# Reading a broadcast scalar through 16 partitions and a ones matmul, in a streaming multiply-add

## The chip, the core and the metric

The kernel runs on one core of a Trainium2 chip. The metric is the device time of one execution in microseconds; the kernel before takes 153.68 us (median of three runs, 153.3 to 153.85). A core has five engines that matter here: TensorE (PE) for matrix multiplications, VectorE (DVE) and ScalarE (ACT) for elementwise work, GpSimd (POOL), and SyncE (SP), which only issues transfers. Transfers between the device's memory and the on-chip memory SBUF (128 partitions) run on 16 DMA engines. SyncE and ScalarE each feed them through a queue of their own, q1 and q10 in this profile. PSUM is the small memory into which TensorE writes its results.

## The reference

```python
B, S, D = 512, 32, 640
x:  (512, 32, 640) bfloat16
fx: (512, 32, 640) bfloat16
alpha: (1,) bfloat16

def reference(x, fx, alpha):
    return x + alpha * fx
```

Each of the three large arrays has 10,485,760 elements, that is 20.97 MB. The kernel has to read two of them and write one, 62.9 MB in all, and does one multiply-add for each element.

## The kernel before

The three arrays are seen as 128 partitions of 81,920 elements each, and this row is cut into K = 5 chunks of 16,384 elements (`CHUNK`). One chunk of one array is 128 x 16,384 x 2 bytes, 4.19 MB, with 32,768 contiguous bytes for each partition.

For chunk k, `load_x(k)` and `load_f(k)` bring x and fx into SBUF tiles `x_t` and `f_t`. `compute(k)` is one VectorE instruction, `scalar_tensor_tensor`, that forms f_t * a_f + x_t and writes it over x_t (line 65). `store(k)` writes x_t to the output. There are four buffers for x_t and two for f_t, so a load of fx for chunk k has to wait until chunk k - 2 has been computed, and the load of x for chunk 4 until chunk 0 has been stored. The last chunk is computed and stored in two halves.

The order of the instructions is written out by hand (lines 81 to 101) and no scheduler changes it. All loads and stores are issued by SyncE in that order, except x of chunk 0, which ScalarE issues: SyncE's queue therefore has alpha, f0, x1, f1, x2, and then, as the computations end, f2, store 0, x3, f3, store 1, x4, f4 and the other stores. A queue passes transfers on in this order, and an issue that has to wait for a buffer holds up those after it on the same engine.

The scalar alpha is needed on all 128 partitions, as the operand `a_f` of each multiply-add. The function `alpha_to_lanes` (line 16) makes it: a transfer on SyncE, ahead of all others, reads the same two bytes once for each of the 128 partitions into `a_b` (line 20), and a VectorE copy turns them into float32 (line 22). Line numbers of 104 and above belong to the start and end of the program.

Of the kernel before, what the change touches and what calls it, by code (L numbers as in the profile page):

```python
# [1 line left out]

# [4 lines left out]

ACT = mybir.ActivationFunctionType
ALU = mybir.AluOpType
F32 = mybir.dt.float32  # L10
BF16 = mybir.dt.bfloat16

CHUNK = 16384


def alpha_to_lanes(nc, consts, alpha, eng):

    P = nc.NUM_PARTITIONS
    a_b = consts.tile([P, 1], alpha.dtype, name="a_b")
    eng.dma_start(out=a_b[:], in_=alpha.to_broadcast((P, 1)))  # L20
    a_f = consts.tile([P, 1], F32, name="a_f")
    nc.vector.tensor_copy(out=a_f[:], in_=a_b[:])  # L22
    return a_f


@with_exitstack
def kernel(
    ctx: ExitStack,
    tc: tile.TileContext,
    x: bass.AP,  # L30
    fx: bass.AP,
    alpha: bass.AP,
    out: bass.AP,
):
    nc = tc.nc
    P = nc.NUM_PARTITIONS
    xv = x.flatten_outer_dims().rearrange("(p n) d -> p (n d)", p=P)
    fxv = fx.flatten_outer_dims().rearrange("(p n) d -> p (n d)", p=P)
    ov = out.flatten_outer_dims().rearrange("(p n) d -> p (n d)", p=P)
    F = xv.shape[1]  # L40
    K = F // CHUNK
    assert K * CHUNK == F and K == 5

    consts = ctx.enter_context(tc.tile_pool(name="consts", bufs=1))
    xs = ctx.enter_context(tc.tile_pool(name="xs", bufs=4))
    fs = ctx.enter_context(tc.tile_pool(name="fs", bufs=2))
    ctx.enter_context(tc.manual_schedule())

    a_f = alpha_to_lanes(nc, consts, alpha, nc.sync)
    xt, ft = {}, {}  # L50

    def load_x(k):
        xt[k] = xs.tile([P, CHUNK], x.dtype, tag="x", name="x_t")
        eng = nc.scalar if k == 0 else nc.sync
        eng.dma_start(out=xt[k][:], in_=xv[:, bass.ts(k, CHUNK)])

    def load_f(k):
        ft[k] = fs.tile([P, CHUNK], fx.dtype, tag="f", name="f_t")
        nc.sync.dma_start(out=ft[k][:], in_=fxv[:, bass.ts(k, CHUNK)])

    def compute(k, parts=1):
        n = CHUNK // parts
        for j in range(parts):
            s = bass.ts(j, n)
            nc.vector.scalar_tensor_tensor(  # L65
                out=xt[k][:, s],
                in0=ft[k][:, s],
                scalar=a_f[:],
                in1=xt[k][:, s],
                op0=ALU.mult,  # L70
                op1=ALU.add,
            )

    def store(k, j=0, parts=1):
        n = CHUNK // parts
        nc.sync.dma_start(
            out=ov[:, k * CHUNK + j * n : k * CHUNK + (j + 1) * n],
            in_=xt[k][:, bass.ts(j, n)],
        )

    load_x(0)
    load_f(0)
    load_x(1)
    load_f(1)
    load_x(2)
    compute(0)
    load_f(2)
    store(0)
    load_x(3)
    compute(1)  # L90
    load_f(3)
    store(1)
    load_x(4)
    compute(2)
    load_f(4)
    store(2)
    compute(3)
    store(3)
    compute(4, 2)
    store(4, 0, 2)  # L100
    store(4, 1, 2)


# [1 line left out]
_INS = ['x', 'fx', 'alpha']  # L105
_OUTS = [((512, 32, 640), 'bfloat16')]


# [23 lines left out]
```

## Time and profile before

| | |
|---|---|
| median of three runs | 153.68 us |
| the profiled execution | 153.68 us |
| its span, first to last instruction | 151.9 us |
| VectorE: four multiply-adds of 128 x 16,384 | 69.1 us, 17.28 each |
| VectorE: two multiply-adds of 128 x 8,192 | 17.4 us, 8.75 each |
| VectorE: copy of alpha to float32 | 0.15 us, at 14.73 |
| VectorE idle until alpha has landed | 14.7 us |
| VectorE idle until an f_t has landed | 38.2 us in five waits |
| bytes read and written | 41.94 MB and 20.97 MB |
| TensorE | no compute instruction |

The idle times are those that ended with the landing named: VectorE had nothing else to do meanwhile. An idle engine costs nothing by itself; what counts is whether the end of the kernel hangs on it. The mean rate of the transfers over the span is 414 GB/s, and the page's slices give the rate over time, in 40 parts of 3.8 us each.

### The profile page before, as it was taken

The page shows a single profiled execution, that of the slowest core. Times are in us where ns is not written, and L with a number is a line of the kernel's source. Part 1 is how long each engine was busy: PE and PEld are TensorE (multiplying, and loading weights), DVE is VectorE, ACT ScalarE, POOL GpSimd, SP SyncE. Part 2 cuts the span into 40 slices and gives each one's busy share as a digit, 9 for nine tenths or more (in the row PEclk, how much of TensorE's full clock was granted, in tenths as well). Part 3 has the DMA queues.
Part 4 walks back from the last instruction along what each step waited for, and adds up shares of the span by engine and source line. Part 5 has one row for each costly group of instructions (what it writes and reads, how often), then busy time and mean ns, then how long its engine had stood idle before and what let it go on. Part 6 is the DMA issues. An engine that isn't in the chain of part 4 may idle for free.

```text
span 151.9 us, 81 instructions
## 1 busy us (share of the span) xinstructions
DVE 86.7 (57%) x7; POOL 0.2 (0%) x4
## 2 busy tenths in 40 slices
DVE  0000005999949999499992005999900089997000
POOL 0000000000000000000000000000000000000000
DMA  6988999999999999999999999999999999999993
GB/s 216 440 328 345 440 423 431 414 440 449 431 440 431 431 414 423 449 449 431 431 423 423 423 414 449 449 431 423 431 423 414 431 466 449 423 423 397 431 419 168
DMA packets 2448, 62.92 MB, mean 414 GB/s; under 512 B 400, under 2 KB 400, under 8 KB 400
## 3 DMA queue, kind: packets, MB, share of 16 engines
q1 hardware_dynamic: 2304, 58.72, 89.9%
q10 hardware_dynamic: 144, 4.19, 7.2%
HBM read 41.94 MB, written 20.97 MB: 414 GB/s over the span
## 4 chain that ended last, share of the span: by engine, by line
DMA 57%; DVE 29%; DVEq 6%; SPq 0%; issue 0%
DMA f_t<-in_fx_dram 57%; DVE x_t L65 29%; DVEq L127 6%; SPq L20 0%; DVEq L65 0%
## 5 line engine op out<-in xcount | busy, mean ns | idle before, releaser
L65 DVE SCALAR_TENSOR_TENSOR x_t<-f_t,a_f,x_t 128x16384 bf16<-128x16384 bf16 (+1 forms) x6 | 86.5, 14439 | 38.2 <-DMA f_t<-in_fx_dram 38.2
L22 DVE CAST a_f<-a_b 128x1 f32<-128x1 bf16 x1 | 0.2, 153 | 14.7 <-DMA a_b<-in_alpha_dram 14.7
L116 POOL MEMSET const-bfloat16-1.0<- 128x1 bf16 x1 | 0.1, 101 | 0.0
L116 POOL MEMSET const-uint8-127<- 128x1 uint8 x1 | 0.1, 101 | 0.0
L116 POOL MEMSET const-float32-0.0<- 128x1 f32 x1 | 0.1, 98 | 0.2 <-issue 0.2
L116 POOL MEMSET const-float32-1.0<- 128x1 f32 x1 | 0.1, 98 | 0.0
## 6 DMA issues: line engine op xcount, KB each, us to landing
f_t<-in_fx_dram SPq DMA_DIRECT2D x5, 4096.0 KB, 31.6
x_t<-in_x_dram SPq DMA_DIRECT2D x4, 4096.0 KB, 39.6
out_dram<-x_t SPq DMA_DIRECT2D x4, 4096.0 KB, 36.0
x_t<-in_x_dram ACTq DMA_DIRECT2D x1, 4096.0 KB, 13.3
out_dram<-x_t SPq DMA_DIRECT2D x2, 2048.0 KB, 13.3
a_b<-in_alpha_dram SPq DMA_DIRECT2D x1, 0.2 KB, 14.0
```

The costliest lines, as they stand in the source:

```text
L22: nc.vector.tensor_copy(out=a_f[:], in_=a_b[:])
L65: nc.vector.scalar_tensor_tensor(out=xt[k][:, s], in0=ft[k][:, s], scalar=a_f[:], in1=xt[k][:, s], op0=ALU.mult, op1=ALU.add,)
L116: nc = _bacc.Bacc("TRN2", target_bir_lowering=False, num_devices=1)
L127: with _tile.TileContext(nc) as tc:
```

## The change

Alpha is now read to 16 partitions instead of 128, by a transfer that ScalarE issues instead of SyncE. One row of it, a single element, is the moving operand of a matmul whose stationary operand is a row of 128 ones, set by VectorE; the product, alpha on 128 partitions, lies in PSUM as float32, and the VectorE copy into `a_f` reads it from there. The load of x for chunk 0 moves from ScalarE's queue to the head of SyncE's; the order of SyncE's other issues is the same. The tiles, the buffers, the multiply-adds and the stores are not touched.

```diff
-def alpha_to_lanes(nc, consts, alpha, eng):
+def alpha_to_lanes(nc, consts, psum, alpha, eng):
 
     P = nc.NUM_PARTITIONS
-    a_b = consts.tile([P, 1], alpha.dtype, name="a_b")
-    eng.dma_start(out=a_b[:], in_=alpha.to_broadcast((P, 1)))
+    a_1 = consts.tile([16, 1], alpha.dtype, name="a_1")
+    eng.dma_start(out=a_1[:], in_=alpha.to_broadcast((16, 1)))
+    ones = consts.tile([1, P], alpha.dtype, name="ones")
+    nc.vector.memset(ones[:], 1.0)
+    a_ps = psum.tile([P, 1], F32, name="a_ps")
+    nc.tensor.matmul(a_ps[:], ones[:], a_1[0:1, :], start=True, stop=True)
     a_f = consts.tile([P, 1], F32, name="a_f")
-    nc.vector.tensor_copy(out=a_f[:], in_=a_b[:])
+    nc.vector.tensor_copy(out=a_f[:], in_=a_ps[:])
     return a_f
...
+    psum = ctx.enter_context(tc.tile_pool(name="psum", bufs=1, space=bass.MemoryType.PSUM))
...
-    a_f = alpha_to_lanes(nc, consts, alpha, nc.sync)
+    a_f = alpha_to_lanes(nc, consts, psum, alpha, nc.scalar)
...
-        eng = nc.scalar if k == 0 else nc.sync
-        eng.dma_start(out=xt[k][:], in_=xv[:, bass.ts(k, CHUNK)])
+        nc.sync.dma_start(out=xt[k][:], in_=xv[:, bass.ts(k, CHUNK)])
```

## The prediction

> **What bounds the kernel now.** I read the page's summary and slices first, since they say which resource is full; then the chain of waits, which says what the end hangs on; then the rate of the DMA engines stretch by stretch, which says where the full resource is not full.
>
> ```profile
> span 151.9 us, 81 instructions
> ...
> DVE 86.7 (57%) x7; POOL 0.2 (0%) x4
> ...
> DMA  6988999999999999999999999999999999999993
> ...
> DMA packets 2448, 62.92 MB, mean 414 GB/s; under 512 B 400, under 2 KB 400, under 8 KB 400
> ```
>
> The only compute engine with work, VectorE, is busy for 57% of the span. The DMA engines read 9 in all slices but the first four (6988) and the last. The last line also says what the alpha read is made of. The kernel issues 17 transfers; if each ends in one small packet on each of 16 engines (the semaphore), that makes 272, and 400 - 272 = 128 packets are left: one 2-byte packet for each partition of a_b, eight on each engine.
>
> The chain of waits, in order of time, of which I show the first part and the end (start us, us, what):
>
> ```profile
> 1.32 23.12 DMA f_t<-in_fx_dram
> ...
> 24.58 17.30 DVE x_t L65
> ...
> 41.89 21.41 DMA f_t<-in_fx_dram
> ...
> 63.39 17.30 DVE x_t L65
> ...
> 80.70 41.33 DMA f_t<-in_fx_dram
> ```
>
> The chain puts 29% on VectorE, but this is a link of time, not a limit. While the multiply-add of tile 0 runs from 24.58 to 41.87, x1, f1 and x2 (three transfers of 4.19 MB) are queued already, 9.7 us each at 432 GB/s, so that the queue runs dry at about 24.5 + 29.1 = 53.6, and f2, the store of tile 0 and x3 join it at 41.9, some 12 us early. So the transfers are one long line, and the bytes set its length. What stands idle in that line is lost; where it is idle is in the table of stretches (columns: stretch, its length, busy time of DVE and of POOL, clock, DMA share, GB/s):
>
> ```profile
> 3.00:5.00 2.00, 0.00 (x0) 0.00 (x0) 1.00 0.95 410
> 5.00:7.00 2.00, 0.00 (x0) 0.00 (x0) 1.00 0.88 377
> 7.00:15.00 8.00, 0.15 (x1) 0.00 (x0) 1.00 0.91 356
> 15.00:31.00 16.00, 6.42 (x1) 0.00 (x0) 1.00 1.01 434
> 31.00:47.00 16.00, 13.90 (x2) 0.00 (x0) 1.00 1.00 432
> 47.00:79.00 32.00, 29.86 (x2) 0.00 (x0) 1.00 1.00 431
> 143.00:149.00 6.00, 0.00 (x0) 0.00 (x0) 1.00 1.01 431
> ```
>
> From 15 us to the end of the stores the engines hold 431 to 434 GB/s, and I take 432 as full. From 7 to 15 us they move 356. That is 8 x (432 - 356)/432 = 1.41 us of the whole line lost there. In the same time alpha and x_0 share the engines, as the page's issues show:
>
> ```profile
> x_t<-in_x_dram ACTq DMA_DIRECT2D x1, 4096.0 KB, 13.3
> ...
> a_b<-in_alpha_dram SPq DMA_DIRECT2D x1, 0.2 KB, 14.0
> ```
>
> Alpha's 256 bytes take 14.0 us from issue to landing and the 4 MB of x_0 13.3 us, against 9.7 us for a transfer of that size at 432 GB/s. The packet records of the trace show how: on each engine three packets of x_0 go first, then one of alpha and one of x_0 in turn. The first two of alpha cost nothing visible (the next 32 KB packet again takes 1.21 us), from the third on x_0's packets take 1.3 to 1.6 us. At the end, near 13 us, alpha's last two or three small packets go through with little beside them, and f_0, queued behind them on the same queue, has not started. That is the hole of 12 to 14 us.
>
> **What the Trainium skill says.** "DMA: Bandwidth & Descriptors", section "Queues, rings and completion order", states that each DMA engine takes the queues that have work in turn, packet by packet; the records agree, one alpha packet to one of x_0. The section "Why a DMA increments its semaphore by 16 and not by 1" gives the number of engines that share a transfer: the largest number up to 16 that divides the slowest dimensions of both sides. So 16 partitions get 16 engines, one element each; the 128 small packets of before (eight per engine) fit that, and no run yet shows the 16-row form. The section "Issuing engines are not separate DMA queues" states that transfers of different issuers run on the same 16 engines, so that moving x_0 from ScalarE's queue to SyncE's buys no bandwidth; the trace agrees, as its rate after 15 us, with SyncE alone issuing, is the 432 above.
>
> **The change part by part.** The sum is made against the profiled execution: 153.68 us, of which 151.9 is the span and 1.8 lies around it. The median of the runs shown is the same 153.68.
>
> *Alpha's read, 128 packets to 16.* Eight 2-byte packets per engine become one. Its cost before is the 1.41 us of the stretch from 7 to 15. What one costs is not shown by itself. Lower bound: nothing, since the first two alpha packets on each engine cost nothing and the 4-byte semaphore packets later lie in the stream without lowering 432. Upper bound: the loss of 3 to 7 us as well was alpha's (2 x 22/432 + 2 x 55/432 = 0.36 us) and returns in full. I take 0. Removed: 1.41 us. Were all of 3 to 15 us alpha's, it would be 1.77.
>
> *Alpha moved to ScalarE's queue, x_0 to SyncE's.* SyncE issues x_0 first, in the place of alpha, then f_0, x_1, f_1, x_2 as before: still five issues at the start, so nothing later is issued later. Alpha's first issue on SyncE took 0.54 us (0.72 to 1.26), x_0's on ScalarE 0.36 (0.73 to 1.09). If SyncE takes 0.54 for x_0, its data starts 0.17 us later; if 0.36, not at all. I take +0.10. All transfers of x and fx are now on one queue, and the engines go from x_0 to f_0 as they go from f_0 to x_1 in before, where the table shows no loss.
>
> *The work added: memset of a 1 x 128 row, weight load and matmul of one column, copy out of PSUM.* None is in the trace of before except the copy (0.153 us, from SBUF); the small memsets of GpSimd took 0.10. For the matmul, "TensorE: Matmul & The Clock Gate", section "Part 2: What happens when you issue a matmul", prices one of N columns at the low clock at (219 + N)/1.2 ns, 0.18 us here, which no run yet shows. By these an estimate of the chain is 0.1 + 0.18 + 0.15, about half a microsecond after alpha lands; with the waits between the engines I allow 2 us. VectorE's first multiply-add waits for x_0 and f_0, which land near 23 us. If alpha lands by 7 us (behind three packets of x_0, the worst order that the trace shows), a_f is ready by 9 with 14 us to spare, and if alpha stayed as late as 14.7 there would still be 6. The matmul waits for alpha and the copy for the matmul; behind the copy on VectorE stands only the multiply-add of tile 0, which would delay f_2 and the store of tile 0, whose issue has those 12 us of cover. Cost: 0. On TensorE, and on ScalarE behind its one issue, nothing is queued.
>
> *What is late next.* Nothing new: the line moves as a whole. f_0 lands 1.3 us earlier, tile 0 ends earlier, f_2 is issued earlier by the same, and the last store too, because each issue has its cover in a full queue (the last half store is issued at 139.7 and the other stores are under way until about 146).
>
> Sum: 153.68 - 1.41 + 0.10 + 0 = 152.37, said as 152.4; with the other bounds 151.9 (1.77 removed, no later start) to 152.9 (1.41 removed, 0.36 and 0.17 back).
>
> **The rivals.**
> *Half of it stays.* One small read per engine still upsets the stream at the start, when x_0's first packets are being waited for. For it: those first packets took 1.7 to 2.4 us, so the start is delicate. Against: two alpha packets in the middle cost nothing. 153.68 - 0.7 = 153.0.
> *No change.* The hole is made by passing from one queue to the other with a small transfer between, whatever its count, or only some engines gain while the slowest stays. For it: the end is set by the slowest of 16 engines, and the last packets of the engines end 1.4 us apart. Against: x_0's packets are slowed well before the passage. 153.6.
> *Slower: SyncE's queue starts late.* Alpha was issued on SyncE's queue at 0.72, yet its first packet runs 4.1 us after the first of x_0, which was issued on ScalarE's at 0.73. If that is the queue's own start and not its turn behind x_0, x_0 now pays it: 153.68 - 1.41 + 4.1 = 156.4. It makes the kernel slower once the late start is more than 1.41 + 0.46 = 1.9 us. Against: alpha enters on every engine exactly after its third x_0 packet, staggered like those packets, which looks like turns behind read-ahead.
> *The change does not do what it says.* Were the 16 reads put on one engine, that engine would have twice the small packets of before, and lose about 2.8 us instead of 1.4: 155.1.
>
> **How the numbers follow.** Full gain, 152.4: 0.60. Half, 153.0: 0.18. No change, 153.6: 0.12. Late queue, 156.4: 0.07. One engine, 155.1: 0.03. A difference of 0.3% (0.46 us) is what a measurement can tell, so faster means under 153.22 and slower over 154.14. Faster: 0.60 and most of the half case, 0.75; same: the rest of that case and the third, 0.15; slower: 0.10. Range: 151.6 (a little under the lower bound, for the spread of the runs, 153.3 to 153.85) to 153.5, which leaves out the slower cases and part of the third.
>
> **What would show it.** Right: 288 packets under 512 B in place of 400; alpha landing within some 7 us; x_0 landing near 11 to 12 us, f_0 and the first multiply-add near 23; 7 to 15 us at about 432 GB/s; all later landings shifted by the same 1.3 us. Wrong: first data after 3 us (late queue), 7 to 15 us still below 400 (no gain), or the early gain there and the last store no earlier (then the bytes are not the line that I take them for).

## The result, and the profile after

| | before | after |
|---|---|---|
| median of four runs each | 153.65 us (153.3 to 153.85) | 152.84 us (152.58 to 152.95) |
| ratio | | 0.9947, 95% interval 0.9925 to 0.997 |
| the profiled execution, its span | 153.68, 151.9 us | 152.80, 151.0 us |

The changed kernel is 0.8 us faster in these runs. A second series, 22 runs of it beside 67 of the kernel before, gave 0.9965 (0.995 to 0.9979), some 0.5 us. The forecast was 152.4, a gain of 1.3 us, so the direction held and the gain is about half of it.

The page of the kernel after, its summary, its slices and its packets:

```profile
span 151.0 us, 85 instructions
...
DMA  6999999999999999899999999999999999998994
GB/s 208 443 434 434 425 417 417 434 443 451 443 434 434 417 417 399 347 460 434 425 434 417 417 417 425 451 469 434 417 443 417 417 425 425 460 469 360 425 443 187
DMA packets 2336, 62.92 MB, mean 417 GB/s; under 512 B 288, under 2 KB 288, under 8 KB 288
```

There are 288 small packets instead of 400, 112 fewer, as 16 reads in place of 128 have to give. The slices at the start are full now: 6999 where before read 6988. But the rates show two low values that the kernel before has nowhere in its middle: 399 and 347, the slices from 56.6 to 64.2 us.

The same in the table of stretches, first before, then after (stretch, its length, busy time of each engine that works, clock, DMA share, GB/s; a packet counts in the stretch in which it starts, so only long stretches are sharp):

```profile
7.00:15.00 8.00, 0.15 (x1) 0.00 (x0) 1.00 0.91 356
15.00:48.00 33.00, 21.32 (x2) 0.00 (x0) 1.00 1.00 434
48.00:72.00 24.00, 21.86 (x2) 0.00 (x0) 1.00 1.00 433
72.00:148.00 76.00, 43.37 (x4) 0.00 (x0) 1.00 1.00 429
```

```profile
7.00:15.00 8.00, 0.16 (x1) 0.00 (x0) 0.16 (x1) 0.00 (x0) 1.00 1.04 446
15.00:48.00 33.00, 0.00 (x0) 0.00 (x0) 23.04 (x2) 0.00 (x0) 1.00 1.00 432
48.00:72.00 24.00, 0.00 (x0) 0.00 (x0) 20.84 (x2) 0.00 (x0) 1.00 1.01 415
72.00:148.00 76.00, 0.00 (x0) 0.00 (x0) 42.67 (x4) 0.00 (x0) 1.00 1.00 430
```

From 7 to 15 us the hole is filled, 446 for 356. From 48 to 72 us there is a new one: 24 x (433 - 415)/433 = 1.0 us.

The chain of waits after, in order of time, shows what this does to the line of transfers:

```profile
1.17 21.55 DMA f_t<-in_fx_dram
...
22.84 17.30 DVE x_t L69
...
40.16 22.44 DMA f_t<-in_fx_dram
...
62.69 17.29 DVE x_t L69
...
80.00 41.03 DMA f_t<-in_fx_dram
...
121.22 8.75 DVE x_t L69
```

The first multiply-add starts at 22.84, 1.74 us earlier than before (24.58). The third starts at 62.69, only 0.70 earlier (63.39): f_2 takes 22.44 us from its issue where it took 21.41. So more than half of the early gain is given back on the way to f_2. By the last chunk the lead is 1.0 us, against this line of the chain before:

```profile
122.22 8.75 DVE x_t L65
```

Of it 0.9 us is in the span of this execution; how far single executions differ is seen under e4.

The new path of alpha is harmless, as the timeline after shows (start, length, engine, line, operation; in brackets the idle time before it and what ended it):

```profile
0.73 0.57 ACTq L20 DMA_DIRECT2D a<-in_alpha_dram  x1
0.73 0.38 SPq L59 DMA_DIRECT2D x_t<-in_x_dram  x1
...
8.19 0.16 PE L24 MATMUL a_ps<-a,ones 1*128 1x1 bf16 x1 [8.19 <-DMA a<-in_alpha_dram]
8.38 0.16 DVE L26 COPY a_f<-a_ps 128x1 f32<-128x1 f32 x1 [7.41 <-PE a_ps L24]
```

Alpha lands just before 8.2 us, and 0.35 us later a_f is there, 14.3 us before the first multiply-add can use it. The issue of x_0 takes SyncE 0.38 us, and by the packet records its first data starts at 1.74 us, where before it was 1.73.

### The profile page after: what moved, and what is told of

It reads as the page before. It is cut to its first block, busy times and chain, and to the rows that moved or that the text cites. A ratio compares the mean times of both kernels' runs of the same rounds, so it can differ in the third digit from the quotient of the medians.

```text
span 151.0 us, 85 instructions
## 1 busy us (share of the span) xinstructions
PE 0.2 (0%) x1; PEld 0.1 (0%) x1; DVE 86.9 (58%) x8; POOL 0.2 (0%) x4
## 4 chain that ended last, share of the span: by engine, by line
DMA 56%; DVE 29%; DVEq 6%; issue 0%; SPq 0%
DMA f_t<-in_fx_dram 56%; DVE x_t L69 29%; DVEq L131 6%; SPq L59 0%; DVEq L69 0%
```

## The experiments

For all of them one measure is read from the timelines: the start of the first multiply-add, and the distance from the second to the third. Between these two lie the landings of f_1 and f_2, that is two transfers of 4.19 MB, 19.4 us at 432 GB/s; what is over 19.4 was lost on the way. Before and after:

```profile
43.96 17.28 DVE L65 SCALAR_TENSOR_TENSOR x_t<-f_t,a_f,x_t 128x16384 bf16<-128x16384 bf16 x1 [2.10 <-DMA f_t<-in_fx_dram]
...
63.39 17.29 DVE L65 SCALAR_TENSOR_TENSOR x_t<-f_t,a_f,x_t 128x16384 bf16<-128x16384 bf16 x1 [2.14 <-DMA f_t<-in_fx_dram]
```

```profile
42.24 17.28 DVE L69 SCALAR_TENSOR_TENSOR x_t<-f_t,a_f,x_t 128x16384 bf16<-128x16384 bf16 x1 [2.11 <-DMA f_t<-in_fx_dram]
...
62.69 17.28 DVE L69 SCALAR_TENSOR_TENSOR x_t<-f_t,a_f,x_t 128x16384 bf16<-128x16384 bf16 x1 [3.16 <-DMA f_t<-in_fx_dram]
```

A landing waits for the slowest of the 16 engines. The mean of the engines is in the column "lost": the transfer time lost in the first 20 us after the first packet, and in the 50 us after that, from the packet records with 433 GB/s as full. Some 0.9 us of the first 20 is the start itself and is lost in e3 too, which reads no alpha: the first packet of x_0 on each engine takes 1.85 to 2.0 us in the mean, the later ones 1.21.

The kernels ran in several series, each beside the kernel before, whose median was 153.37 to 153.65; the ratio is to that of the same series. "Small packets" are the 2-byte reads of alpha on each engine ahead of the first store.

| kernel | small packets per engine | first multiply-add | second to third | third | lost: first 20 us, next 50 | median us | ratio to before, interval |
|---|---|---|---|---|---|---|---|
| before | 8 | 24.58 | 19.43 | 63.39 | 2.47, 0.00 | 153.65 | |
| after | 1 | 22.84 | 20.45 | 62.69 | 0.88, 1.11 | 152.84 | 0.9947 (0.9925 to 0.997) |
| e1 swap only | 8 | 24.18 | 19.44 | 63.01 | 2.21, 0.02 | 153.23 | 0.9998 (0.9983 to 1.0013) |
| e2 count only | 1 | 22.99 | 20.06 | 62.45 | 0.90, 0.80 | 153.00 | 0.9974 (0.9949 to 1.0) |
| e3 no alpha | 0 | 22.67 | 20.36 | 62.44 | 0.88, 0.87 | 153.08 | 0.9977 (0.9961 to 0.9994) |
| e4 after again | 1 | 22.96 | 20.29 | 62.64 | 0.92, 0.91 | 152.86 | 0.9965 (0.995 to 0.9979) |
| e5 delay | 0 | 23.71 | 20.11 | 63.22 | 0.89, 0.83 | 153.82 | 1.0023 (1.0001 to 1.0045) |
| e6 longer delay | 0 | 25.18 | 20.13 | 64.71 | 0.88, 0.84 | 155.56 | 1.0142 (1.0095 to 1.0188) |
| e7 store 0 late | 0 | 23.00 | 19.41 | 61.82 | 0.93, 0.85 | 153.00 | 0.9972 (0.9956 to 0.9988) |
| e8 mid read | 1, then 8 | 22.88 | 20.70 | 62.99 | 0.94, 1.25 | 153.68 | 1.001 (0.999 to 1.003) |
| e9 before and mid read | 8, then 8 | 24.51 | 19.51 | 63.43 | 2.44, 0.11 | 153.81 | 1.0033 (1.0013 to 1.0053) |
| e10 early write | 1, and 1 write | 22.90 | 20.00 | 62.30 | 0.93, 0.71 | 153.03 | 0.9972 (0.9954 to 0.9991) |
| e12 64 partitions | 4 | 23.18 | 19.68 | 62.25 | 1.19, 0.52 | 152.77 | 0.9974 (0.9948 to 1.0) |

**e1 and e2: one half of the change each.** e1 has only the queues swapped:

```diff
-    a_f = alpha_to_lanes(nc, consts, alpha, nc.sync)
+    a_f = alpha_to_lanes(nc, consts, alpha, nc.scalar)
...
-        eng = nc.scalar if k == 0 else nc.sync
-        eng.dma_start(out=xt[k][:], in_=xv[:, bass.ts(k, CHUNK)])
+        nc.sync.dma_start(out=xt[k][:], in_=xv[:, bass.ts(k, CHUNK)])
```

> Only the queues are swapped: alpha still goes to 128 partitions (eight 2-byte packets on each engine), now from ScalarE's queue, and x_0 heads SyncE's. Theory A (the small packets between x_0's slow the stream, wherever they come from): the loss of 7 to 15 us stays whole, first multiply-add near 24.5 us, time 153.3 to 153.8. Rival B (the order on SyncE's queue: f_0 stands behind alpha and can't start while alpha's last small packets trickle): f_0 now follows x_0 directly, the hole of 12 to 14 us (about 0.55 us) goes but x_0's packets stay slow (about 0.7), first multiply-add near 23.7, time about 153.0. Rival C (moving x_0 to SyncE's queue makes the whole gain): first multiply-add at 22.8, time 152.8.

e2 has only the new way of reading alpha, on the old queue:

```diff
-    a_f = alpha_to_lanes(nc, consts, psum, alpha, nc.scalar)
+    a_f = alpha_to_lanes(nc, consts, psum, alpha, nc.sync)
...
-        nc.sync.dma_start(out=xt[k][:], in_=xv[:, bass.ts(k, CHUNK)])
+        eng = nc.scalar if k == 0 else nc.sync
+        eng.dma_start(out=xt[k][:], in_=xv[:, bass.ts(k, CHUNK)])
```

> Only the count is changed: alpha goes to 16 partitions with the ones matmul, but still at the head of SyncE's queue, with x_0 on ScalarE's. Theory A: 16 packets instead of 128, so the early gain is whole: first multiply-add at 22.8 us, 7 to 15 us at 430 GB/s or more, time 152.8. Rival B (queue order) and C (x_0's queue): most of the loss stays, first multiply-add at 23.5 to 24.5, time 153.2 to 153.7.

The first multiply-add starts at 24.18 in e1 and 22.99 in e2, between 24.58 and 22.84. By itself the swap brings 0.4 us of the early gain, the count 1.6. The 0.4 fits rival B, in which f_0 no longer stands behind alpha's last small packets, but it is not shown: e3 and e7, which start alike, differ by 0.33 in this measure. The early gain comes from the count. In the time this is less sharp: the median of e1 cannot be told from before, and that of e2 is 0.4 us lower with an interval that ends at 1.0.

**e3: no alpha at all.** A memset of a constant takes the place of alpha's read, the matmul and the copy; x_0 heads SyncE's queue.

```diff
-    a_1 = consts.tile([16, 1], alpha.dtype, name="a_1")
-    eng.dma_start(out=a_1[:], in_=alpha.to_broadcast((16, 1)))
...
+    nc.vector.memset(a_f[:], 0.005)
```

> Alpha is not read at all (a_f is set by a memset to 0.005), x_0 heads SyncE's queue: alpha's read and the matmul are left out. Theory A with one read per engine costing nothing: the same early stretch as after, first multiply-add at 22.8 us, time 152.8. Rival (the one read that is left still costs): first multiply-add at 22.4 or earlier and 0.3 to 0.5 us less, 152.3 to 152.5.

22.67 and 153.08: no faster than after. One small read per engine costs nothing that the median shows. The dip of the middle, as the loss near 60 us is called from here on, is there too (20.36), so it needs neither alpha nor the matmul.

**e4: the changed kernel once more.**

> The changed kernel once more, for a second trace. In the first, the transfers lost about 1.1 us between 56 and 62 us, with packets of up to 2.1 us, which the kernel before does not show there. Theory D (the dip belongs to the changed order and gives the early gain back): the dip is there again at 56 to 62 us, and time is 152.8. Rival E (dips come and go from run to run, in every kernel): the dip is elsewhere, smaller or missing in this trace, the last store moves by its size, and the time of single runs spreads by some tenths of a us around 152.8.

The dip came again in the same place, 20.29 for 19.43. It belongs to the changed kernel: theory D. The packet records of this trace put it on the last two packets of f_2 on every engine: from the mean of 1.22 us they go to 1.38 and 1.95 us, and the first store's packets after them are back at 1.21.

The median of the 22 executions is 152.86, but the traced one took 153.69, the longest of them. Its last multiply-add starts at 122.11, for 121.22 in the first trace, so that the lead over the kernel before is nearly gone there. Its last packets end 1.7 us apart, those of the first trace 0.8, while the mean of the engines ends only 0.2 us later: one late engine sets the end. A single execution can thus lose as much as the whole gain, in part as rival E has it, and what arrives at the end is told by medians and not by one trace.

**e5 and e6: time or place?** The kernel of e3 (alpha left out) with a memset that holds up x_0's load, of 1,536 elements and, in e6, of 4,096:

```diff
         xt[k] = xs.tile([P, CHUNK], x.dtype, tag="x", name="x_t")
+        if k == 0:
+            nc.vector.memset(xt[k][:, :1536], 0.0)
```

> The kernel without alpha's read (e3; alpha left out, a_f a constant), with a VectorE memset of 1,536 elements for each partition of x_0's tile ahead of x_0's load, so that everything starts later by the memset's length, some 0.4 to 1.6 us. Measured against the start of the transfers, theory F (the loss at the passage from f_2 to the first store belongs to this flow of transfers, wherever it lies in time): a dip of 0.8 to 1.1 us on f_2's last two packets again, time 153.08 plus the whole delay. Rival G (it hangs on the time since the start of the program, and the kernel before passes that place too late): with the first multiply-add near 24 us the dip is gone, and time is 153.08 or less in spite of the delay.

> As the run before, with a memset of 4,096 elements (1 to 4.3 us). Theory F: the same dip, time 153.08 plus the whole delay. Rival G: no dip at f_2's end, time 153.08 plus the delay less 0.9 us.

In e5 the first load is issued at 1.71 instead of 0.73, in e6 at 3.05. The multiply-adds of e6 in its timeline:

```profile
25.18 17.28 DVE L64 SCALAR_TENSOR_TENSOR x_t<-f_t,a_f,x_t 128x16384 bf16<-128x16384 bf16 x1 [22.16 <-DMA f_t<-in_fx_dram]
...
44.58 17.29 DVE L64 SCALAR_TENSOR_TENSOR x_t<-f_t,a_f,x_t 128x16384 bf16<-128x16384 bf16 x1 [2.11 <-DMA f_t<-in_fx_dram]
...
64.71 17.28 DVE L64 SCALAR_TENSOR_TENSOR x_t<-f_t,a_f,x_t 128x16384 bf16<-128x16384 bf16 x1 [2.85 <-DMA f_t<-in_fx_dram]
```

The first now starts later than in the kernel before, and still 64.71 - 44.58 = 20.13; in e5 20.11 (43.11 to 63.22). The dip does not hang on the time since the start, over these 2.3 us. The medians, 153.82 and 155.56, are those of e3 plus 0.74 and 2.48, about the 0.98 and 2.32 by which the first load is late. Theory F holds.

**e7: move the first store.** The kernel of e3 (alpha left out) with

```diff
     load_f(2)
-    store(0)
     load_x(3)
+    store(0)
```

> The kernel without alpha's read (alpha left out), with the store of chunk 0 issued after the load of x_3 in place of ahead of it, so that x_3 follows f_2 and the first write to the output comes one transfer (9.7 us) later. Theory F: the dip moves with the first passage from loads to a store, to the last packets of x_3 at 66 to 70 us, and f_2 lands 0.9 us earlier, at 61.5. Rival G (time since the start): the dip stays at 57 to 61 us. Time about 153.1 in both, unless the dip needs exactly the old order and vanishes, then 152.2.

```profile
23.00 17.28 DVE L62 SCALAR_TENSOR_TENSOR x_t<-f_t,a_f,x_t 128x16384 bf16<-128x16384 bf16 x1 [22.14 <-DMA f_t<-in_fx_dram]
...
42.41 17.29 DVE L62 SCALAR_TENSOR_TENSOR x_t<-f_t,a_f,x_t 128x16384 bf16<-128x16384 bf16 x1 [2.12 <-DMA f_t<-in_fx_dram]
...
61.82 17.29 DVE L62 SCALAR_TENSOR_TENSOR x_t<-f_t,a_f,x_t 128x16384 bf16<-128x16384 bf16 x1 [2.13 <-DMA f_t<-in_fx_dram]
```

In this timeline f_2 lands with no loss, 61.82 - 42.41 = 19.41. In the packet records the slow packets are now the last two of x_3, with means of 1.57 and 1.67 us, one transfer later, and the median is the same. The dip goes where the first passage from loads to a store goes.

**e8 and e9: the same small packets in the middle.** A second read of alpha to 128 partitions is issued by ScalarE when the first multiply-add has ended, in e8 in the changed kernel, in e9 in the kernel before. Its result is not used.

```diff
     store(0)
+    a_2 = consts.tile([P, 1], alpha.dtype, name="a_2")
+    nc.vector.tensor_copy(out=a_2[:], in_=xt[0][:, 0:1])
+    nc.scalar.dma_start(out=a_2[:], in_=alpha.to_broadcast((P, 1)))
     load_x(3)
```

> The changed kernel with a second read of alpha to 128 partitions, from ScalarE's queue when the multiply-add of chunk 0 has ended, near 40 us, where the engines run at 432 GB/s and nothing waits for it. It prices the 128 small packets by themselves, without the start and without anything behind them on their queue. Theory A (small packets between large ones slow the stream): the transfers lose 1.0 to 1.6 us in the 10 us after 41, time 153.9 to 154.4. Rival B (the loss came from what stood behind alpha on SyncE's queue, or from the start): under 0.3 us is lost there and time stays within 153.1.

> The kernel before, with the same second read of alpha to 128 partitions near 42 us as in e8. Theory H (the stream has one reserve, which the first disturbance uses up, be it alpha's small packets or the first store; so the losses don't add): the read near 42 us costs much less than the 0.73 us of e8, 0.2 or less, there is no dip at f_2's end, and time is within 0.3 of the kernel before. Rival A2 (128 small packets cost 0.7 us wherever they are): 0.6 to 0.8 us lost from 42 to 52 us, time 0.7 over the kernel before.

The second and third multiply-adds, in the timeline of e8 and then of e9:

```profile
42.29 17.29 DVE L69 SCALAR_TENSOR_TENSOR x_t<-f_t,a_f,x_t 128x16384 bf16<-128x16384 bf16 x1 [1.93 <-DMA f_t<-in_fx_dram]
...
62.99 17.28 DVE L69 SCALAR_TENSOR_TENSOR x_t<-f_t,a_f,x_t 128x16384 bf16<-128x16384 bf16 x1 [3.42 <-DMA f_t<-in_fx_dram]
```

```profile
43.92 17.29 DVE L65 SCALAR_TENSOR_TENSOR x_t<-f_t,a_f,x_t 128x16384 bf16<-128x16384 bf16 x1 [1.93 <-DMA f_t<-in_fx_dram]
...
63.43 17.29 DVE L65 SCALAR_TENSOR_TENSOR x_t<-f_t,a_f,x_t 128x16384 bf16<-128x16384 bf16 x1 [2.23 <-DMA f_t<-in_fx_dram]
```

In e8 the distance is 20.70, 1.28 us lost. By the packet records 0.74 of it is lost between 40 and 50 us after the first packet, at the small packets, and 0.52 from 50 to 60, at the dip, which is smaller than without them. Both expectations missed: 0.74 lies between theory A's 1.0 and rival B's 0.3, and so does the median between their times. In e9, where the kernel has had its 128 small packets at the start, the same 128 packets cost 19.51 - 19.43 = 0.08, and there is no dip. So the losses do not add: what the small packets have taken, the first store does not take again, nor do further small packets. That is theory H in its main point. One part of its expectation missed: the median of e9 is 0.44 us over the kernel before, between theory H's 0.3 and rival A2's 0.7, so the second read is not free in the time. The trace does not show where that goes: its last multiply-add starts at 122.28, for 122.22 before.

**e10: a first write, early.** The changed kernel with 16 rows of 512 bytes of zeros written to the output's last columns, which the last store overwrites:

```diff
+    z = consts.tile([16, 256], x.dtype, name="z")
+    nc.vector.memset(z[:], 0.0)
+    nc.scalar.dma_start(out=ov[0:16, F - 256 : F], in_=z[:])
```

> The changed kernel with a write of 16 rows of 512 bytes of zeros into the output's last columns at the start (the last store overwrites them). Theory W (the dip is the cost of the first write to the output as such): the dip at f_2's end goes, time 152.0. Theory H (it is the passage of the stream from loads to stores): the dip of 0.8 to 1.1 us stays, time 152.8 to 153.0.

The write was issued at 8.7 us; the dip stayed, 20.00. It is not the price of the first write as such. It is the smallest dip of the kernels with one read or none, 0.6 us by this measure and 0.7 by the packet records, under the 0.8 that theory H expected; whether its one more small packet per engine is the reason is not shown.

**e11: stores beside the loads.** The changed kernel with `nc.scalar.dma_start` in `store`.

> The changed kernel with all stores on ScalarE's queue, so that the first store's packets come in turn with those of the loads in place of behind f_2. Theory H (a passage from loads to stores drains the reserve, and one packet of each in turn does so as well): a loss of 0.5 to 1.1 us, now near 42 us where the first store is issued, time within 0.3 of 152.9. Rival (the dip needs the whole stream of an engine to turn from loads to stores at once): no dip, time 152.0, and a kernel that beats both.

165.77 us, 1.0816 (1.0784 to 1.0847): both expectations of the time missed, for a reason that neither had in view. The rates of e11 over its slices (4.1 us each):

```profile
GB/s 248 392 424 472 384 496 400 408 488 384 384 408 432 432 440 424 416 448 432 416 432 440 440 448 400 432 448 416 440 432 432 432 424 392 0 0 320 192 256 256
```

Stores and loads take turns, so the stores are done early and the loads late; the third multiply-add starts at 80.59 instead of 62.69, the last at 139.32, and while its first half is computed (8.7 us) nothing is left to transfer: two slices at 0.

```profile
139.32 17.41 DVE L69 SCALAR_TENSOR_TENSOR x_t<-f_t,a_f,x_t 128x8192 bf16<-128x8192 bf16 x2 [20.35 <-DMA f_t<-in_fx_dram]
```

In the hand-written order the older stores, still waiting behind the loads, fill just this gap. As to the dip, 0.87 us were lost here from 40 to 50 us after the first packet, when the first store had been issued, and nothing from 50 to 60 (packet records): in this trace a passage in turns costs about the same as one at once.

**e12: four packets per engine.** The changed kernel with 64 for 16 in `a_1` and its read.

> The changed kernel with alpha read to 64 partitions in place of 16: four small packets on each engine, between one (after) and eight (e1). Theory H (one reserve, spent once): what the packets take early, anything from 0 to 0.7 us between 7 and 15, is missing from the dip at f_2's end, so that the loss by 60 us is the same 1.7 to 2.0 us as with one packet; time 152.7 to 153.0. Rival A2 (each packet beyond the first costs its own share and the dip is separate): about 0.5 us early and a full dip of 0.8 to 1.1, loss by 60 us 2.3 or more, time 153.3 to 153.5.

```profile
23.18 17.29 DVE L69 SCALAR_TENSOR_TENSOR x_t<-f_t,a_f,x_t 128x16384 bf16<-128x16384 bf16 x1 [10.64 <-DMA f_t<-in_fx_dram]
...
42.57 17.28 DVE L69 SCALAR_TENSOR_TENSOR x_t<-f_t,a_f,x_t 128x16384 bf16<-128x16384 bf16 x1 [2.11 <-DMA f_t<-in_fx_dram]
...
62.25 17.28 DVE L69 SCALAR_TENSOR_TENSOR x_t<-f_t,a_f,x_t 128x16384 bf16<-128x16384 bf16 x1 [2.40 <-DMA f_t<-in_fx_dram]
```

By the landings 0.5 us is lost early (23.18 against e3's 22.67, but 0.2 against e7's 23.00) and only 0.27 at the dip (19.68 - 19.41), where e3 loses 0.95. The packet records, which don't hang on the slowest engine, have 0.3 more lost early than in e3 and 0.52 at the dip, so that what comes early is missing later. The losses of both columns sum to 1.71, as theory H expected; the rival's 2.3 or more did not come. The median, 152.77, is that of one packet, though its interval reaches up to the kernel before.

Over all the kernels of the table, this sum is 1.6 to 2.0 us with none, one or four small packets per engine, and 2.2 to 2.55 with eight or more. Four packets take only what the first store would take in any case; eight take some half a microsecond more. That half microsecond is about what the medians gain.

## Why the prediction was right in direction and too large

*What bounds the kernel: right.* The transfers are one line: the lead of 1.0 us at the last chunk is 0.9 in the span, and the delays of e5 and e6 came out at the end nearly whole.

*What the 128 small packets cost at the start: a little low.* The sum took 1.41 us from the stretch of 7 to 15 us, with 1.77 as the upper bound. The first multiply-add moved by 1.74, the packet records have 1.59 (2.47 - 0.88).

*What one packet per engine costs: right,* nothing that can be measured (e3 against after). The change also does what it says: the 16 reads came as 16 packets of 2 bytes that all started within 0.75 us, 4.1 us after the first of x_0, and not one after the other on one engine.

*x_0 on SyncE's queue: the term of +0.10 was not there.* SyncE issues x_0 in 0.38 us, ScalarE did in 0.36. The rival of a late queue fell with it: x_0's data starts as early, and alpha, now on ScalarE's queue, again enters 4.1 us after x_0's first packet, behind three packets of x_0. That delay is a matter of turns and not of the queue. The Trainium skill's "DMA: Bandwidth & Descriptors", section "Queues, rings and completion order", has the turns, and the trace before agrees: the first packets of alpha start at 5.85 us, the second ones at 7.07, with one packet of x_0, 1.21 us, between. The three packets ahead of the first turn are what the traces of both kernels add.

*Matmul, copy, and alpha's landing: right,* with 0.35 us for the chain (the matmul 0.16, for an estimate of 0.18) and 14 us to spare. Alpha landed at 8.2 and not by 7.

*"What is late next. Nothing new: the line moves as a whole."* This is the step that failed: it put at nothing what the transfers lose later. f_2 became late, by 1.0 us, at the passage to the first store. The kernel before has no loss there, nor has e1 with its eight small packets per engine, and e8 and e12 have a smaller one: what small packets have lost is not lost again. The gain is therefore not what alpha cost at the start, but what it cost beyond the loss that comes in any case: by the third multiply-add 1.74 - 1.02 = 0.7 us, and 0.5 to 0.8 in the medians of the two series.

*The rival "half of it stays"* came near with 153.0, but for a reason that is not the one seen: the one small read at the start upsets nothing (e3); the loss comes back near 60 us. That the forecast of this rival fits the time so well is luck.

*Three slips in the working, none of which carries the forecast.* The upper end of the sum comes to 153.68 - 1.41 + 0.36 + 0.17 = 152.80, not 152.9. The engines do not hold 431 to 434 GB/s to the end of the stores: from 111 to 143 us the rate before is 427. And the queue would run dry at 52.2, not 53.6, since x_1 was under way when the first multiply-add began; the packet records have f_2's first packet there, so the cover is 10 us instead of 12.

What stays open is what this one loss is. The runs show that it is 0.7 to 1.1 us by the packet records where no more than one small read precedes it, that it falls on the last two 32 KB packets of each engine ahead of the first store, and that it is missing or smaller after four or eight small packets. It is not that small packets merely set the engines out of step: the ends of x_2, the transfer ahead of f_2, lie 0.71 us apart over the 16 engines in e1, which has no dip, and 0.72 after and 0.35 in e3, which have it. A stock of data read ahead, which the first disturbance uses up, would behave so; no run shows such a stock itself.

## What to carry to other kernels

Where the transfers bound a kernel, a fill in the rate early on is worth only what is still there at the last transfer: compare the lead at several landings, not the hole that was closed. A broadcast of a few bytes to 128 partitions ahead of a stream is eight small reads on each DMA engine; read it to fewer partitions and spread it on chip, if the engine for that is idle; here that was worth 0.5 to 0.8 us of 153.7. And losses found one at a time may not add: put both into one kernel before summing them.

## What the runs showed of the hardware

- The first passage of the DMA engines from loads to stores cost 0.9 to 1.1 us in the two traces of the changed kernel; in the kernel before, after 128 small reads, nothing. All that came later, up to 140 us after the first packet, cost 0.1 to 0.4 us together in these three traces.
- Small packets and this passage did not add: 128 small reads in the middle of the stream cost 0.74 us in e8, and about 0.1 in e9, where 128 had come before.
- A broadcast read of 2 bytes took its queue 0.53 to 0.61 us to issue for 16 or 64 partitions and 0.52 to 0.54 for 128, on either queue. That is within what the loads of 128 rows of 32 KB took (0.33 to 0.65): its small size buys nothing there.
- A second queue does not get its first turn at once: its first packet came 4.1 us after the other queue's, behind three packets of 32 KB on each engine, whichever queue was which. In mid-stream it was alike: the second read of e8, issued at 40.39, had its first packet at 44.87.
